# Another order table for a block-sparse attention with a gated FFN on one core

## The chip, the cores and the metric

The kernel runs on one core of a Trainium2 chip. A core has a matrix engine (TensorE, PE in the profile; its weight loads are listed as PEld), a vector engine (DVE), a scalar engine (ACT), a GpSimd engine (POOL) and a sync engine (SP). Each engine works through its own instruction stream strictly as written, and engines wait for each other through semaphores. DMAs are issued from SP, ACT or POOL and run beside the engines. The metric is the device time in microseconds (us). Three runs of the kernel before took 215.96, 216.22 and 216.23 us; the median is 216.22.

## The reference

Four sequences of 768 positions, 8 heads of 64 features. Attention is masked by blocks of 32 positions: a block sees its neighbours, the first and the last block, and three random blocks per row, which are given at run time.

```python
scores = scale * np.matmul(q, k.transpose(0, 1, 3, 2))
...
scores = np.where(mask, scores, -1000000000.0)
...
attn = attn / (np.sum(attn, axis=-1, keepdims=True) + 1e-09)
return np.matmul(attn, v).astype(np.float32)
```

The heads are put side by side (512 features) and go through a gated feed-forward layer with a convolution of width 3 over the positions:

```python
h = np.maximum(x @ w_in, 0.0)          # 512 -> 1024
...
conv_out += conv_w[k][None, None, :] * hp[:, k:k + S, :]
gate = 1.0 / (1.0 + np.exp(-conv_out))
return (h * gate @ w_out).astype(np.float32)   # 1024 -> 512
```

## The kernel before

**The work.** The kernel computes dense scores and adds the mask through 24 extra rows of the contraction (88 rows instead of 64). Heads are taken in 16 pairs; a pair's keys and queries lie in tiles `e` and `o` (even and odd 128-blocks), its values in `vt`. Queries are taken in halves of 384 positions, so there are eight half batches; the last one is cut into 256 and 128 positions. Scores come in 144 units of 128 keys x 1024 score columns:

- a score step (`s`, L742) is half a unit on PE and writes half of one of two `st` buffers; six matmuls make a unit;
- an exponential (`exp`, L753) on ACT turns a unit from `st` into one of six `pt` buffers;
- an `av` step (L775) on PE multiplies four 128-blocks of `pt` with the values into one of two `av` buffers; a ones column gives the row sums.

18 units make a half batch, and 4.5 units one pair of heads in it. Then follow, for each pair, `rcp` and `norm` on DVE (L692, L694), which divide by the row sums into `xtok`, and a transpose into `xT`: on PE with a copy behind it (`x_tr`, L713, `x_cp`) in the half batches 0, 1, 7 and 8 (the two pieces of the last count as 7 and 8), by a DMA from SP (`x_xb`, L703) in the others.

The feed-forward part of a half batch runs while the next half batch's attention runs: `f1` on PE (L864, eight groups of 128 hidden features, into one of two `mix` buffers), `relu` on ACT (L884) or DVE (L886) into `hE`, then for each pair of groups three `mul` steps (L916) and two `add` steps (L924) on DVE for the convolution, `tanh` on ACT (L963), `g1` and `g2` on DVE (L966, L971) into `gT`; then `f2` on PE (L802), a copy out of PSUM (`ev`, ACT or DVE, L336 or L340) and the output DMA from SP (L809). The last 128 positions have their convolution on PE (`conv`).

**Loads.** The first pair comes as float32 by DMAs from SP and ACT; all others are cast by DMAs issued from POOL (L239). Pairs 0 to 5 are turned by PE transposes (`k_tr`, L466; `q_tr`, L504) with copies behind them (`k_cp`, `q_cp`; L336 on ACT, L340 on DVE); pairs 6 to 15 by DMA transposes from SP (`xb`, L581) and a copy (`stg_cp`). The mask rows are copied from slot to slot on DVE (`m_h1`, `m_slot`, all L340). POOL holds its loads back with one-element copies (`pace`, L414 and L656), which wait for an exponential or an earlier load.

**What sets the order.** The source builds a graph of 1758 steps. Each names the engines that may run it, what it needs, and the buffers it takes and frees. No scheduler runs at build time: the string `ORDER` (L20) lists all steps, two characters for the step, then a letter for the engine where there is a choice (A for ACT, V for DVE), then a digit for each buffer that the step takes. `put_down` (L94, called at L987) reads the string from front to back and writes out each step's instructions. So the string fixes three things: the order of steps on each engine, the engine of each copy, `relu` and `ev`, and which buffer each step gets. A step that stands behind another on a different engine does not wait for it for that alone; it waits for what it needs and for its buffers.

Of the kernel before, what the change touches and what calls it, by code (L numbers as in the profile page):

```python
# [25 lines left out]
6o15yV6p690Z6d6e6q05+16t04v1P05/V6i6j6u6k06y16l6v14w6z160+6m06r06s6A26nV6D00S6E0X4xhW12l06F3hZ00/6I16JhX4y2m6K4
h+hYV06R06Sh/Vi316T5i4ii06W14z176Xik6wi5Ai00iji16Y04A2x11Q1i2V6/0701RAil4B6x2116B7417111SV6C75iq1290im6G762ic1
2aV47d0idir7ein7i14C2bV2z26H7j7f36L6M1is2c04DieV6U6V6Z7k46+7n06N12eV7oit2217p5722dV7s17t24V2n023V7u0737x0iu7y2q1
2oV02B02A7z1777G16O7H784E2pV2F27g0iv7h7L07926P0io4F7l2H37M7I27a7m7q7rip07v7w7A7N37B16QV17Q12rV7R7J0W7K7b07S47V0
7C07W2kV47O2sV7X57D2C4G82183107P7E17T8407cV8707FV887Uiw7Y8918c1ix2J12I7Z8d2yV0i602GV18e28h04H7+12N08i7/i7i918j3  # L30
4Ii8V2f0ia8508m12DV1ibA8nif08o4igiy28u0iz868a8vihAiA2P8z12Q18A8w5iBiO1iG3800iP8B0iC8E02K4J2t18biH8f8FiDiI8J12S8g
8kiJ8l81A8K8piE8q18G18x8yiK2g08CiF8D2RiL8H2iViQ2hV2OA28IiMiU02EViV8L2iN2T0iW2LV2iR2X2Y18R0iSA08SiX8T38W1iYV18X
i+18Y4i/2MV8/090j0Vj109158r2941958sj22Uj71960j3V9909a8Mjm0j409b12+9h1jo2/08t29i8Njnj89j2j58O0jp9m09nj9V8U0j6A8V
319r1jq9o3ja1jbju1jd0jvjrje8P9s9w0jcAjx8Z321308+92jfA93jwjj19t49xjC2jg0jhjyiZ9y5369E1js372jkjiV9798jz9cjE9F2u0jD
9d19G09J0jA9k9KjF9l9L19e19O1jt9p9q339PjlV9u2wA9T02vAjB9U9vk819Q2jK3k9jL9z9V3jGjY0393a29Y19f9A9ZjHjMa409g9H09IjN
9M9+4jZjOa59N9R8QjI9SjP9W3c9XjJa91aaa65kajQiT9/jRj+3bab09B2ae09Cj/2VV3af9Dk0A2kb3h2WVaj1ag1k20a11a2k33d0kcA3k4
2ZA3k5jS1k6V1a30jT34V4akjUal2ar0k1jVa01asjWA0ke0kfat3jXkh1kgV1kiaw135V3kkjAax3l3kn0ay4kokC03i0kk1kEaB0kpAklkDaC
kmAa7kFa8acaG1aD5kq0kGadaHkK1kt1kH3nahkMaL0kr3o13mkLaI0aikuksVamaMkvAkNkz03eaN1aT1kOaUkw1kS2ankPkx3skIkAao0kTaY0
aV2aZkJ1au0avazaAkyVaEkBAaFaJb11kVa+3b2aKkQl61apaOb34b60kRaqb7lc0kUb85be1k+3bfl7l03pbg0aP1kWaWbj0bkaQ2aXk/kXa/b0
b4bo1aRb5b9bl1bal1aSbh0bpldkYl2bq2bt0bikZbubmbb1l3lebcby1bzbv3bdl4bnl8l5brbsbA43qV0bG0bHk7l938V43fV1bI5lf3v3w1  # L40
laV2bL1bMlgA0bwbQ03rVli1bN0lh3gVljll0kdlkV3jA0lm3AbRlblnVbV1bWbS1lr1lG0lo0lIlsbX23x3B1lplHc10c2ltV3t1lqAbxc61lJ
c33c7bBbC1lO1lx1lylKc84cb0bJlzVcclD0lLlQcg1bKlP3ychlu1cd5bD0lRbObPlvbEbTci0lElMcl0bF1lSbUcmlwAbY3KlNct13L0lTlA1
lW2bZculYcn1c40lB3zlXc5c9calFVcv33Hcy03I2czb+2lUcelZlCAmg03PlVcA4cD1cfcEl+mh3Mb/cF2cjcI0ck3uV1ma1c0m23l/cJcom3
cp1cQ1cRcK5m4cw3CcxcBm5cCcGmbcS0m0m6cV0cHcLm1cM3NcWm7c+1cq1micrcX1c/m8mccscN0m9cT0cUd03d30cOd4mjcPd54cY3Zmd3+2
mkV1d81d9meV0mm03Q0da5dg03DV2mn3JV2mo3EV423OcZmfdhd1mpdi03W3Gdl1mqV3dmmy1dn1mz3/mB0mC3X0mAA0dq0mDVd2drms1mW0ds2
mtmX3Rdv1dwmYmudx3mZmE0mv40m+431d6d7mwV2mFm/dD0dbmGVdEdI1dc1n0dF4mH1n10mIdJdd2mJAmN04cde4d3dN0dK5mOn21df2dj41dO
n3dkmK1n4dP0mL494a1n5domxdpdS1dTmPVmMA4hdtdudX0dU13SV3dYdy3TVmQ1mRdZ2n6e314e4i0e4na2dzmT0nbe53mUmSVdG0e80dHe9n7
mVVdLed1dA1eeni3ea4nw1dBdMdQdRncdVef5dCdWd+ei04fndejnq0n8ek0e00eq1neer3Fd/1n9e6e744es1ev0njewnrnkex3eA1e1eb3VeB
ecnlege2nfehel4gem3YV3et0eF0nmeC4nx4ong4p2eueyen2eznheGnneK1eonyeH5eLepnonsnpeDeEeM045V4eS0eT4jnteU2eX1nuV0eYnz
eZ14bV4eI48eJnAV2eNf00mrf1eO1eP1f5146Vf23mlf6nC0eQ47nDf74nI1eR0nEVnJfd04qV0nKAfe4kV1nL0ff5nM3Ufi1nNVnvfjnF14lV  # L50
fk0eV4nnGo60eWnBfn0fonHAo8nR0fp2nSo7fs1n+1e+e/ftnTAn/nO1fu1nPo9fx0o0fyf3nQAf4o1nU0fz3fF1oafGf8f9o2nVfH4nX1oe2fg0
fK0offLo3nYogfhfP1fa0fM5flnZVfQfmfqo4frfbobfU0o5fvfcfVnWAohoA1fR0ocfwou0om3fAodfW2g01g1onfB1fIovoig21g50oog6oBop
ojfJfNfC2fOoqfSg73fTga1fDgbfXfYokfEg30org4g8olg9gj0gkgc4osoCotowgl5fZ1go1f+gpoxgq0f/gdoDoyV3gt0gugeoM0gv24mgf0oN
ggozoOoEA1oPoFgC1oQA0gDgh1gH0giA1gIoS0gE1oToV1oUV1gJ3oWgM1oXVgNp20gO4p3pe1p51pgp6p4Apfgm1gV0p7AgngrphoY0oZpigW
o+Agso/1pu0pjp0pwoG0pvp1Ag+1g/gX5oHpm2oIpnh00oJpogwh30pph4oKA2gxpxpb1h52gF0pqoLpcp80gy2pkoRgGpdAgKgzgLgPhc1prpy
# [962 lines left out]
```

## Time and profile before

| | |
|---|---|
| median of three runs | 216.22 us |
| span of the profiled execution, first to last instruction | 213.9 us |
| what lies around the span (difference of the two) | 2.3 us |
| PE busy | 203.6 us (95%) |
| ACT busy | 193.5 us (90%) |
| DVE busy | 186.6 us (87%) |
| POOL busy | 60.4 us (28%) |
| TensorE clock granted | 1.000 |
| start of the first score step, of the first exponential | 6.8, 7.9 us |
| start of the last exponential | 193.9 us |
| last instruction of PE, of DVE, of ACT | ends at 210.3, 208.4, 210.9 us |

The profiled execution's own time is its span, 213.9 us; its total is not listed apart from the three runs. Busy time is the union of the intervals of an engine's instructions. On PE neighbouring matmuls overlap in the record: `st` matmuls are listed with some 230 ns, but six of them take 0.44 us together.

### The profile page before, as it was taken

Reading aid. Unit: us, or ns where it says so; the run is one execution under the profiler, and the core shown is the slowest. Engines: PE = TensorE matmul, PEld = TensorE weight load, DVE = VectorE, ACT = ScalarE, POOL = GpSimd, SP = SyncE. Lnnn points to the kernel's source line nnn. Section 1 sums busy time; section 2 is a strip of 40 time slices with the busy share of each in tenths; the row PEclk is TensorE's granted clock in tenths of the full one; section 3 lists DMA queues with packets and bytes.
Section 4 is the critical chain, followed back from the end, with each engine's and each line's share of the span. In section 5 each row is a group of like instructions: output and inputs, shape, how many; then the busy total and the mean of one; then the engine's idle time right before and its main releaser. Section 6 shows DMA issues by size and latency. Waiting matters only on the chain.

```text
span 213.9 us, 6829 instructions
## 1 busy us (share of the span) xinstructions
PE 203.6 (95%) x2702; PEld 154.0 (72%) x2721; DVE 186.6 (87%) x577; ACT 193.5 (90%) x252; POOL 60.4 (28%) x117
## 2 busy tenths in 40 slices
PE   7899999999999999999999999999998999999991
PEld 3679978887677775778776766787786867785740
DVE  4899989999989994999999978999799939999980
ACT  6999999999899997999999977999999988997642
POOL 8883455733323130500327152730000000000000
PEclk9999999999999999999999999999999999999999
DMA  6999898998888977693599869699941130200205
GB/s 181 186 195 202 132 123 119 113 172 99 99 123 99 138 133 162 122 106 74 103 234 96 116 104 188 105 143 114 134 154 23 20 122 3 98 5 21 80 0 196
DMA packets 48935, 24.81 MB, mean 116 GB/s; under 512 B 35120, under 2 KB 45832, under 8 KB 48904
## 3 DMA queue, kind: packets, MB, share of 16 engines
q0 software_dynamic: 19728, 11.05, 43.0%
q1 hardware_dynamic: 28888, 13.05, 30.0%
q8 instruction: 21, 0.34, 0.7%
q10 hardware_dynamic: 288, 0.30, 0.4%
q14 instruction: 10, 0.08, 0.1%
HBM read 23.08 MB, written 6.29 MB: 137 GB/s over the span
## 4 chain that ended last, share of the span: by engine, by line
PE 66%; DVE 24%; ACT 6%; issue 3%; ACTq 0%; DVEq 0%
PE st L742 19%; PE mix L802 16%; PE mix L864 12%; PE av L775 10%; DVE m L916 9%; ACT pt L753 4%; DVE m L924 4%; DVE hE L886 3%; PE st L802 2%; PE mix L504 2%; PE av L230 2%; DVE xtok L694 1%; DVE gT L971 1%; DVE o L340 1%; DVE e L340 1%
## 5 line engine op out<-in xcount | busy, mean ns | idle before, releaser
L753 ACT ACTIVATE pt<-st 128x1024 bf16<-128x1024 f32 x144 | 141.3, 1027 | 5.6 <-PE st L742 4.2
L775 PE MATMUL av<-vt,pt 128*128 128x65 bf16 x1152 | 60.4, 193 | 0.2
L775 PEld LDWEIGHTS <-pt 128*128 128x128 bf16 x1152 | 52.3, 97 | 10.1
L864 PE MATMUL mix<-xT,winb 128*128 128x384 bf16 (+2 forms) x288 | 52.8, 308 | 0.3 <-DVE hE L886 0.3
L916 DVE TENSOR_SCALAR m<-hE,cw 128x382 bf16<-128x382 bf16 (+2 forms) x192 | 49.4, 320 | 0.2
L802 PE MATMUL mix<-woutb,gT 128*128 128x512 bf16 x157 | 44.6, 379 | 1.6 <-DVE gT L971 0.6
L742 PE MATMUL st<-o 88*128 88x128 bf16 (+1 forms) x240 | 44.5, 229 | 0.3 <-ACT pt L753 0.2
L742 PE MATMUL st<-o,e 88*128 88x128 bf16 (+1 forms) x228 | 44.2, 233 | 0.2 <-ACT pt L753 0.2
L742 PE MATMUL st<-e,o 88*128 88x128 bf16 (+1 forms) x224 | 42.5, 234 | 1.2 <-ACT pt L753 1.1
L742 PE MATMUL st<-e 88*128 88x128 bf16 (+1 forms) x208 | 41.8, 239 | 0.4 <-ACT pt L753 0.2
L742 PEld LDWEIGHTS <-o 88*128 88x128 bf16 x464 | 34.3, 97 | 8.9 <-issue 2.0
L742 PEld LDWEIGHTS <-e 88*128 88x128 bf16 x436 | 32.9, 97 | 9.0 <-issue 0.9
L924 DVE TENSOR_TENSOR m<-m 128x764 bf16<-128x764 bf16 (+2 forms) x64 | 33.8, 533 | 0.3
L864 PEld LDWEIGHTS <-winb 128*128 128x128 bf16 x288 | 24.2, 97 | 8.2 <-issue 0.8
L963 ACT ACTIVATE m<-m 128x764 bf16<-128x764 bf16 (+2 forms) x32 | 26.3, 821 | 1.9 <-DVE m L924 1.8
L414 POOL COPY pace<-pt 1x1 bf16<-1x1 bf16 x24 | 7.6, 315 | 58.9 <-ACT pt L753 58.8
L802 PEld LDWEIGHTS <-gT 128*128 128x128 bf16 x192 | 15.7, 97 | 11.7 <-DVE gT L971 2.3
L886 DVE TENSOR_SCALAR hE<-mix 128x384 bf16<-128x384 f32 (+2 forms) x30 | 16.4, 553 | 7.9 <-PE mix L864 7.6
L884 ACT ACTIVATE hE<-mix 128x384 bf16<-128x384 f32 (+2 forms) x34 | 16.5, 492 | 3.1 <-PE mix L864 2.2
L971 DVE TENSOR_TENSOR gT<-m,hE 128x764 bf16<-128x764 bf16 (+3 forms) x36 | 18.3, 511 | 0.5
L694 DVE TENSOR_TENSOR xtok<-av,rcp 128x384 bf16<-128x384 f32 (+2 forms) x36 | 18.2, 507 | 0.4
L239 POOL DMA_DIRECT2D nat<-in_q_dram x23 | 16.9, 734 | 2.4 <-issue 1.9
(88 smaller groups left out, 170.0 us busy)
## 6 DMA issues: line engine op xcount, KB each, us to landing
out_dram<-o2s SPq DMA_DIRECT2D x24, 256.0 KB, 2.6
nat<-in_k_dram POOLq DMA_DIRECT2D x15, 192.0 KB, 4.0
vn<-in_v_dram POOLq DMA_DIRECT2D x15, 192.0 KB, 5.5
nat<-in_q_dram POOLq DMA_DIRECT2D x6, 192.0 KB, 4.2
winb<-in_moe_w_in_dram POOLq DMA_DIRECT2D x2, 512.0 KB, 8.4
woutb<-in_moe_w_out_dram POOLq DMA_DIRECT2D x4, 256.0 KB, 4.8
nat<-in_q_dram POOLq DMA_DIRECT2D x9, 96.0 KB, 5.4
nq<-in_q_dram POOLq DMA_DIRECT2D x6, 96.0 KB, 4.5
```

The costliest lines, as they stand in the source:

```text
L239: return op(name, {eng: occ}, lambda e: on(e).dma_start(out=dst(), in_=src), prio, deps, dma=(kind, service), **kw)
L694: nm = op("norm", {"DVE": t_dps(128 * C)}, lambda e: nc.vector.tensor_tensor(out=xtok_t[xk.index][:, 0:C].rearrange("p c h d -> p h c d"), ...
L742: nc.tensor.matmul(out=st[:, 128 * x:128 * (x + n_)], lhsT=QK[kc % 2][s][0:88, 1, hh, kc // 2, :], rhs=QK[par][s][0:88, 0, hh, idx:idx + n ...
L753: nc.scalar.activation(out=pt_t[ptb.index], in_=st_t[stb.index], func=AF.Exp, bias=0.0, scale=0.125)
L775: nc.tensor.matmul(out=o[:, off:off + 65], lhsT=pt_t[ptb.index][:, 128 * x:128 * x + 128], rhs=V_t[vslot_b[P].index][:, hh, kc, 0:65], sta ...
L802: nc.tensor.matmul(out=acc(), lhsT=gT_t[gb.index][:, ffc, 128 * t:128 * t + 128], rhs=woutb[:, ffc, :], start=(ffc == 0), stop=(ffc == NFF ...
L864: nc.tensor.matmul(out=mix_t[hb.index][:, w1 * y:w1 * y + w1], lhsT=winb[:, fc, 128 * ffc:128 * ffc + 128], rhs=xT_t[xt_buf[n].index][:, f ...
L886: nc.vector.tensor_scalar(out=dst, in0=src, scalar1=0.5, scalar2=0.0, op0=ALU.mult, op1=ALU.max)
L916: nc.vector.tensor_scalar(out=m_t[cb.index][:, x, y, 0:w], in0=hE_t[heb.index][:, f0 + y, t0 + x:t0 + x + w], scalar1=cw[:, x, f0 + y:f0 + ...
L924: nc.vector.tensor_tensor(out=m[:, a_, :, 0:w], in0=m[:, a_, :, 0:w], in1=m[:, b_, :, 0:w], op=ALU.add)
L963: th = [op("tanh", {"ACT": t_act(2 * w) + 0.04}, lambda e, cb=cb, w=w: nc.scalar.activation(out=m_t[cb.index][:, 0, :, 0:w], in_=m_t[cb.in ...
L971: nc.vector.tensor_tensor(out=gT_t[gtb.index][:, f0:f0 + 2, t0:t1], in0=m_t[cb.index][:, 0, :, 0:w], in1=hE_t[heb.index][:, f0:f0 + 2, 1 + ...
```

## The change

All but the first 59 steps of the string are replaced: the same 1758 steps in another order, with other engines for some of them and other buffers. The 59 steps that stay are those up to and including the first score step. Nothing else in the source changes.

```diff
 ORDER = """
 000m010g0f0n0h02030410o0i0t050p0j0q0s060zA1t00k0r070AA0l081u18A1090v1F00a0b1aA0c1H20d0N0w01bA19V1c00O0xA1i11f0
-1dV00yA0e1jV1l11eV1kA1gA0R1o00E4K11hA4L0D4P01nA1mV1B14Q4M01v10u0Q0P1I1wV14R14U11xV4V1T11y00G4W24Z01V34+1zV0F1AA
-1W5214/30H532521p11sV05445b02715c1qV1C00I1rA4N0125g15d55h1DV4O4S1J14r1GV1281EV5i04T4X1KV25l05m134Y1LV1M05n15q14s
...
+1dV00yA0e1jV1l11eV1kA1gA0R1o00E4K11B11I4L4P04Q1v02730Q1nA0P0D0G1hV1mV1T11V14M04R10F4U14V1y11sV04Z04N04O4+4S4T
+4W24X5214Y1wV11zV1AA1xV534/31p15445b05c5d50J0I0H1rV0T1qV1C01DV1GV11EV0S4r284s1W5g15h1J15i0505l05m5n11M05q15r
...
```

Steps by engine, where there is a choice (a step not listed keeps its engine):

| step | ACT before | ACT after | DVE before | DVE after |
|---|---|---|---|---|
| relu | 34 | 31 | 30 | 33 |
| ev | 13 | 15 | 11 | 9 |
| x_cp | 5 | 7 | 11 | 9 |
| k_cp | 2 | 1 | 12 | 13 |
| q_cp | 7 | 6 | 19 | 20 |
| v_cp | 3 | 2 | 13 | 14 |
| stg_cp | 0 | 1 | 20 | 19 |

The numbers of instructions are the same on PE (2721 matmuls) and POOL and SP; DVE has 578 for 577, ACT 252 for 253.

The order on DVE from the first mask copy of head 1 on (`m_h1`) begins as follows; the number behind a tile is its buffer in the build, and the columns are the line, the operation, the tiles and the shape written:

```
before                                        after
L340 o_72<-o_72 24x2x384                      L340 o_72<-o_72 24x2x384
L340 e_67<-e_67 24x2x384                      L367 vt_80, L367 vt_79
L340 e_67<-av_64 64x256                       L340 e_67<-e_67 24x2x384
L290 ident_126<-ident 24x24                   L340 o_73<-o_72 24x1536
L367 vt_80, L367 vt_79                        L340 o_72<-av_63 64x384
L340 e_68<-mix_66 64x768                      L340 e_67<-av_64 64x256
L340 o_73<-mix_66 64x768                      L340 e_68<-e_67 24x1536
L340 o_73<-o_72 24x1536                       L340 vt_77<-m_110 128x12x64
L340 e_68<-mix_65 64x2x256                    L340 e_68<-mix_65 64x768
L340 e_68<-e_67 24x1536                       L340 e_68<-mix_66 64x2x256
L340 e_69<-e_67 24x1536                       L340 o_73<-mix_65 64x768
```

On ACT the copy `o_72<-av_63` (64x384, ahead of the first exponential) and the copy `e_67<-mix_66` (64x2x128, ahead of the sixth) are gone; both are on DVE. On PE the `av` steps of units 0, 1 and 2 stand between the score steps of units 3 and 4; before, they stood behind those of unit 5. On POOL the load of pair 3's keys is put ahead of pair 2's values, that of pair 4's keys, with a `pace` copy behind it, ahead of pair 3's queries, and both halves of the first weight matrix (`winb`) behind pair 3's values. Later in the table `norm` of the second pair of half batch 3 (counted from 0) stands behind that of the third pair, and on SP transposes and outputs are interleaved in another order.

More of the change, by code (lines that the diff above doesn't have):

```diff
@@ L26 @@
[L26 to L55, printed above, removed]
@@ new lines @@
+2LV22MVj0V2OA28Y4j2j3Vjm0jnjojp915941952Q32S2R4J2X2Y12t18Ij719909a9609b1j408M9h19i2+2/08Nj8j5jq8O08U08V8Z8+92
+9m09n9j23130j6Ajrj9V8Pju1jvjwjsjd1jx9r1jeja09s9397jbjt2T09o3jfAjy9t4jg1jcA369w09x9y5372989c9d19E19F8t29e1jC29k
+jj0jh9J09l9p9q9K9G09fjDjEjiV2U8Q9gjk9u9O19P9v9z2u1jz9L1iT9Q29A9T09UjlVjY09H09I9MjFjK32vA321iZ339V3jM2wVjGjL9Y1
+k819N9Z9R9S9Wa409Xa5jAjH9+4jNjBk9jZjOjP9B2jIjJa919/aaa65kaj+ab0jQjRae0kbkcA29Ca109D2VV32ZV3afaj1a01j/k0V3a22WA
+ag139k21k3k4jS0jTakjUjVk5ar0al234V4jWV0k6A1asa7ke0kfkh1kikgV1kjVkC0kDkE3a23c3bkFkGat3aw1axkn0aB0ay4a303d0a8ko
@@ L61 @@
+hP4pYApQ1hHqu2hnhJ0qihKqvqwpRpSho0hpA2pThI1hL0hMVhQhRqjpUA1hx0pPpVozhyAhS2hThU1q00hVAqR1qSqTAq1q60qkq7q8qO1qP
+r30q9qaq2Ar4qbr53qU0qVqWAqlqQVqcqdqm1qnr6qxq+1qoqX1q/r00r1qYqZAqpr2qqqI0qJqyr7qC1rd0reqDr81rf0qrqsqtqzqAr9ri0
+ro1rprjra3qKqEqBqFrgrhrbrcqGA3qLqHqMV2qNrqrrrsA1rtrkrlrmA0rn
 """
```

36 lines of the change are left out of this document (29 added, 7 removed).

## The prediction

> **What bounds the kernel now.** I read the page first (busy shares, slices, chain, groups), then the waits, then the span cut at the first exponential of each half batch, then the instructions around the point where the two tables part.
>
> ```profile
> PE 203.6 (95%) x2702; PEld 154.0 (72%) x2721; DVE 186.6 (87%) x577; ACT 193.5 (90%) x252; POOL 60.4 (28%) x117
> ...
> PEclk9999999999999999999999999999999999999999
> ...
> PE 66%; DVE 24%; ACT 6%; issue 3%; ACTq 0%; DVEq 0%
> ...
> L753 ACT ACTIVATE pt<-st 128x1024 bf16<-128x1024 f32 x144 | 141.3, 1027 | 5.6 <-PE st L742 4.2
> ```
>
> Three engines are nearly full at once. No single one carries the chain that ended last; it changes between PE and DVE and touches ACT.
>
> ```profile
> 25.90:46.00 20.10, 19.82 (x325) 16.77 (x322) 18.30 (x65) 19.60 (x24) 11.72 (x23) 1.00 1.05 120
> 46.00:70.20 24.20, 23.96 (x306) 17.95 (x306) 22.18 (x66) 23.53 (x31) 8.43 (x16) 1.00 0.90 117
> 97.00:120.10 23.10, 22.63 (x322) 17.51 (x323) 22.62 (x66) 22.98 (x30) 7.90 (x14) 1.00 0.81 130
> 120.10:143.90 23.80, 23.59 (x303) 17.50 (x304) 21.25 (x58) 20.91 (x25) 10.20 (x19) 1.00 0.94 130
> 193.90:213.90 20.00, 15.20 (x128) 9.08 (x127) 13.62 (x55) 10.09 (x22) 0.00 (x0) 1.00 0.21 79
> ```
>
> Each row is a stretch; its length, then busy PE, PEld, DVE, ACT and POOL. In 97 to 120 all three have under 0.5 us to spare; in 120 to 144 PE binds and ACT has 2.9 us free; in the last 20 us none is full, that is the tail.
>
> ```profile
> DVE hE L886 <- PE mix L864: 7.6, 8, 2.8
> ...
> ACT pt L753 <- PE st L742: 4.2, 10, 1.0
> ...
> ACT m L963 <- DVE m L924: 1.8, 3, 1.4
> ```
>
> No wait is large: the longest on ACT is 1.4 us. What a new order can win are many small waits, and it can make some.
>
> ```profile
> 7.22 0.76 ACT L336 COPY o<-av 64x384 bf16<-64x384 bf16 x2
> 7.88 2.84 ACT L753 ACTIVATE pt<-st 128x1024 bf16<-128x1024 f32 x3
> 8.95 0.22 PE L742 MATMUL st<-e,o 88*128 88x128 bf16 x1 [0.74 <-ACT pt L753]
> ...
> 12.85 0.37 ACT L336 COPY e<-mix 64x256 bf16<-64x256 bf16 x1
> 13.12 1.96 ACT L753 ACTIVATE pt<-st 128x1024 bf16<-128x1024 f32 x2
> ```
>
> Two copies stand ahead of the first exponential on ACT, one ahead of the sixth.
>
> **Work by engine.** PE's work is the same; POOL and SP issue the same DMAs. ACT gives up three `relu` (0.39 each, from start to next start), a `k_cp` (0.49), a `q_cp` (0.27) and a `v_cp` (0.80) and takes two `ev` (0.48), two `x_cp` (0.36) and one `stg_cp`. That copy of 64x1536 has no row on ACT; by exponentials (1024 columns, 0.92) and `ev` (512, 0.48) it is between 0.92 and, continued on their line, 1.36, and I take 1.36. Sum: -2.73 + 3.04 = +0.3, and with the cheaper shapes among them about 0. DVE changes by 0.2. So all that can move the time is waiting.
>
> **The start, walked by hand.** DVE after its mask copy (ends 7.4 with head 1's E copy behind it at 7.8) now does a slot copy (0.55), the copy taken from ACT (0.32), the query copy (0.24): 8.91. Then slot copy (0.55) and the value copy (0.75): 10.21. On ACT the first exponential needs the scores that end at 7.44 and starts at 7.5 instead of 7.88; the third needs score steps that wait for DVE's 8.91 and starts at 9.6 (before 9.7). Then the new order costs: `av` of unit 0 stands ahead of the second score step of unit 3 and waits for the values, 10.21, so exponential 3 (counted from 0) starts at 10.94 (before 10.89); unit 4 waits for pair 1's key and query copies, 10.21 + 0.47 + 0.33 + 0.47 = 11.48, so it starts at 11.98 (before 11.81). Without the ACT copy exponential 5 starts at 12.90 (before 13.12). Three slot copies, two query copies and two fills now hold `mix` until 13.8, so the next key transposes come at 13.85 and exponential 7 at 15.1 (before 15.19); DVE's copies for pair 2 end at 16.25 and exponential 9 starts at 16.97 (before 17.23). **Gain 0.3.**
>
> **DMAs moved.** Pair 3's queries, issued at 8.70 before, now stand behind pair 4's keys and a `pace` that waits for pair 0's queries, which landed at 11.3: issue about 11.9, with this kind's median of 5.4 us to landing 17.3. Their transposes ran at 19.0, by the walk 18.7: hidden, 1.4 us left of 4.1. Pair 2's values go behind one more load of 0.72 us, having 4.2 us to spare. The first weights move from 12.1 to about 14.3, landing (8.4) 22.7, first `f1` 28.6: hidden. Pair 0's second queries had landed 0.3 us before their transposes at 11.6; these now run near 11.8. SP's queue keeps its 20 + 20 transposes; the tightest `f1` (104.4, three us after its last `xT` issue) has 1.1 us more PE work ahead of it. Zero for all of these.
>
> **The middle.** For each half batch I add up, from the first unit to the next half batch's first, the durations of the steps that stand there on PE (between score steps) and on ACT (between exponentials), by the spacings in the trace: a unit of scores 0.44, four `av` matmuls 0.12, four `f1` 0.65, two `f2` 0.43, exponential 0.92, `tanh` 0.73.
>
> | units | from, us | took | PE before/after | ACT before/after |
> |---|---|---|---|---|
> | 0-18 | 7.9 | 18.0 | 14.8/15.0 | 17.1/16.8 |
> | 18-36 | 25.9 | 20.1 | 18.1/18.3 | 18.9/19.3 |
> | 36-54 | 46.0 | 24.2 | 22.2/21.7 | 23.1/21.9 |
> | 54-72 | 70.2 | 26.8 | 26.1/26.3 | 24.4/24.6 |
> | 72-90 | 97.0 | 23.1 | 21.3/21.7 | 22.7/22.3 |
> | 90-108 | 120.1 | 23.9 | 23.7/23.2 | 19.9/22.9 |
> | 108-126 | 144.0 | 22.2 | 20.8/21.0 | 21.4/20.7 |
> | 126-143 | 166.2 | 27.7 | 25.5/25.5 | 24.9/24.6 |
>
> The larger of the two, summed from unit 18 on, goes from 161.4 to 159.5: -1.9. With marks every 36 units it stays (0.0), every 9 it rises by 0.7. These are the ends; they differ in how much lead an engine may have over another, which no row gives, so I take their mean: **gain 0.4**. DVE has 1.2 to 4.3 us free in the same stretches but for 97 to 120.
>
> **The tail.** Behind the last score step PE has 16.2 before and 16.1 after; behind the last exponential ACT 8.8 and 8.5; behind the last `norm` DVE 9.4 and 9.2; `f2`, `ev` and output close it in the same order. **Gain 0.1.**
>
> **Sum.** Span 213.9 - 0.3 - 0.4 - 0.1 = 213.1; with 2.3 around it (216.22, the median, less the span) 215.4 us.
>
> **Rivals.**
> 1. *No net change.* The start's 0.3 is swallowed by the first stretch where PE binds (120 to 144) and the middle stays at its 36-unit sum: 216.2.
> 2. *Slower: `tanh` waits for DVE's adds and holds the exponentials behind it.* Place: units 66 to 92. Six of the eight `tanh` there start at most 0.12 us after the add that they need (89.06 after 89.03; those at 92.1, 97.9, 110.3, 113.4 and 121.3 alike). The new table has 0.8 to 2.7 us less ACT work ahead of the eight and 0.8 to 1.6 us more DVE work ahead of their adds. Where DVE did not do this extra work in its idle time before (3.7 us free between 70 and 97, mostly waits for `f1`), they come up to 1.6 later: 216.2 + 1.6 = 217.8. It decides once DVE's free time in that stretch is under 1.6. For it: chain pieces on DVE at 85.0 to 90.6 and 105.9 to 117. Against: those 3.7 us. If the same happens before units 136 and 139 (adds with 1.7 to 2.0 us more in front), another 1.0 is lost: 218.8.
> [...]
> 4. *Late loads.* Pair 3's queries took 6.2 us to land when issued at 8.70. At 11.9 + 6.2 = 18.1 they still come before 18.7; what goes beyond that is lost on the path: 1.5 us later than 18.7 makes the forecast's 215.4 into 216.9.
>
> **Chances.** Forecast, with the middle anywhere in its gain: 0.50. No net change 0.12. Rival 2: 0.30; rival 4 and the like in SP's queue: 0.06; clock: 0.02. Runs of one kernel differ by some 0.1%, so 0.2% (0.43 us) is about what can be told from no change. Faster 0.50, within 0.2% 0.12, slower 0.38. Low end: 0.5 at the start, 1.9 in the middle and a fifth of the 7.5 us that the stretches take beyond their larger load (1.5): 212.3. High end: rival 2 at both places, 218.8. For the forecast alone 213.5 to 215.8.
>
> **What would show it.** Right: first exponential near 7.5, the tenth near 17.0; the first exponential of half batch 3 (before 70.2) and of half batch 6 (144.0) 0.3 to 1 us earlier; the tail 20 us. Wrong: `tanh` with idle of over 2 us from adds in the waits, or the stretch from unit 72 to 90 over 23.6 us; idle on PE from `gT` above its 0.6.

## The result: 0.7% slower

The changed kernel takes 217.76 us (median of 20 runs, 217.12 to 219.56), the kernel before, run between them, 216.93 us. The ratio is **1.0069, 95% interval 1.0046 to 1.0092**: 1.0 to 2.0 us slower, where 0.8 faster was forecast. A later series of 12 gave 218.78 us and 1.0083 (1.0050 to 1.0117). One sentence is needed to read these numbers: the medians are over all executions and the ratios leave out the slowest ones, which are mostly the old table's (43 of its 149 in all series lie above 219.7 us, none of the new table's 32), so that 0.7% is the difference of undisturbed executions, while the means over all of them are 217.9 us before and 218.0 after in the first series, 217.9 and 218.7 in the later one.

The profiled execution after took 217.51 us, its span is 215.6 (before 213.9). The page of after, the lines that answer to those of before and one more, L802:

```profile
PE 204.8 (95%) x2700; PEld 155.2 (72%) x2721; DVE 186.6 (87%) x578; ACT 192.8 (89%) x251; POOL 61.0 (28%) x117
...
DVE 43%; PE 42%; ACT 10%; issue 4%; ACTq 0%; DVEq 0%
...
L753 ACT ACTIVATE pt<-st 128x1024 bf16<-128x1024 f32 x144 | 142.3, 1033 | 5.4 <-PE st L742 4.3
...
L802 PE MATMUL mix<-woutb,gT 128*128 128x512 bf16 x155 | 43.3, 379 | 2.5 <-DVE gT L971 1.5
```

The engines do nearly the same work as before. In the chain DVE's share has risen from 24% to 43% and PE's has fallen from 66% to 42%, and TensorE now waits 1.5 us for the DVE's gating products `gT`, 0.6 before. The same five stretches, cut at the first exponentials of the same half batches in after (columns: stretch, length, busy PE, PEld, DVE, ACT, POOL, clock, DMA share, GB/s):

```profile
26.50:47.60 21.10, 20.14 (x324) 17.01 (x321) 18.78 (x68) 19.69 (x25) 11.09 (x24) 1.00 1.02 124
47.60:70.70 23.10, 22.66 (x305) 17.25 (x303) 22.28 (x64) 22.28 (x29) 8.65 (x17) 1.00 0.85 106
98.50:121.20 22.70, 22.24 (x319) 17.53 (x323) 22.48 (x68) 22.53 (x29) 7.41 (x13) 1.00 0.67 120
121.20:145.90 24.70, 24.33 (x319) 18.22 (x320) 20.22 (x55) 23.65 (x30) 10.99 (x19) 1.00 0.94 128
196.10:215.60 19.50, 14.70 (x129) 8.91 (x128) 13.01 (x53) 9.58 (x22) 0.00 (x0) 0.98 0.26 95
```

Units 18 to 36 take 1.0 us more (21.1 for 20.1), units 36 to 54 1.1 less, 72 to 90 0.3 less, 90 to 108 0.8 more, the tail 0.5 less (the rows are cut at tenths of a microsecond). The list of waits of after (engine and line, what it waited for, sum, times, longest):

```profile
PEld L802 <- DVE gT L971: 3.2, 8, 1.0
...
ACT o L336 <- DVE e L340: 1.2, 2, 0.8
...
DVE o L340 <- ACT e L336: 0.9, 1, 0.9
...
ACT m L963 <- DVE m L924: 0.9, 3, 0.4
```

The list of before has, for TensorE's matmuls that wait for `gT` (1.5 us in the L802 row of after) and for copies on one engine that wait for copies on the other:

```profile
PE mix L802 <- DVE gT L971: 0.6, 2, 0.3
...
DVE e L340 <- ACT o L336: 0.3, 1, 0.3
```

New in size in after are the second and the third row, 2.1 us between copies on ACT and copies on DVE (0.3 in before); the fourth is shorter than it was. L336 and L340 are one helper, a copy on ACT or on DVE. A transposed query tile is copied in two halves, `q_cp`; where one half is on ACT and the other on DVE, the second waits until the first is done (in after it starts 0.03 us behind the first one's end, at 35.26 and at 41.11). Before has five such pairs too and after six, so it is not the split alone that costs, but what stands ahead of the first half and behind the second. In the timeline of after, DVE and then ACT (start, duration, instruction, idle time before it and what ended it):

```profile
33.81 0.54 DVE L916 TENSOR_SCALAR m<-hE,cw 128x382 bf16<-128x382 bf16 x2
35.26 0.42 DVE L340 COPY o<-mix 64x512 bf16<-64x512 bf16 x1 [0.91 <-ACT e L336]
```

```profile
39.29 1.02 ACT L753 ACTIVATE pt<-st 128x1024 bf16<-128x1024 f32 x1 [0.16 <-PE av L775]
41.11 0.37 ACT L336 COPY o<-mix 64x256 bf16<-64x256 bf16 x1 [0.79 <-DVE e L340]
41.38 1.02 ACT L753 ACTIVATE pt<-st 128x1024 bf16<-128x1024 f32 x1
```

At 35.26 the DVE has stood idle 0.91 us for ACT's half (`q_cp13`); it then works without a break to 41.1, so its half `q_cp18` comes late, and ACT waits 0.79 for it with `q_cp19`, and with `q_cp19` exponential 30. Before has one row of five exponentials there:

```profile
36.66 5.01 ACT L753 ACTIVATE pt<-st 128x1024 bf16<-128x1024 f32 x5
```

From exponential 24 to 30 before takes 7.25 us, after 8.62. (Steps are numbered from 0 in the order in which the kernel defines them; exponential u is unit u's.)

### The profile page after: what moved, and what is told of

It reads as the page before. It is cut to its first block, busy times and chain, and to the rows that moved or that the text cites. A ratio compares the mean times of both kernels' runs of the same rounds, so it can differ in the third digit from the quotient of the medians.

```text
span 215.6 us, 6829 instructions
## 1 busy us (share of the span) xinstructions
PE 204.8 (95%) x2700; PEld 155.2 (72%) x2721; DVE 186.6 (87%) x578; ACT 192.8 (89%) x251; POOL 61.0 (28%) x117
## 4 chain that ended last, share of the span: by engine, by line
DVE 43%; PE 42%; ACT 10%; issue 4%; ACTq 0%; DVEq 0%
DVE m L916 15%; PE mix L802 12%; PE st L742 11%; ACT pt L753 9%; DVE m L924 9%; PE mix L864 8%; DVE hE L886 5%; PE av L775 4%; DVE xtok L694 3%; DVE gT L971 3%; DVE o L340 2%; DVE e L340 2%; DVE m L966 2%; PE av L230 2%; PE st L802 2%
## 5 line engine op out<-in xcount | busy, mean ns | idle before, releaser
L775 PE MATMUL av<-vt,pt 128*128 128x65 bf16 x1152 | 58.2, 193 | 0.2
L775 PEld LDWEIGHTS <-pt 128*128 128x128 bf16 x1152 | 51.1, 97 | 8.8 <-issue 0.4
L864 PE MATMUL mix<-xT,winb 128*128 128x384 bf16 (+2 forms) x288 | 53.5, 308 | 0.4 <-DVE hE L886 0.3
L802 PE MATMUL mix<-woutb,gT 128*128 128x512 bf16 x155 | 43.3, 379 | 2.5 <-DVE gT L971 1.5
L742 PE MATMUL st<-e,o 88*128 88x128 bf16 (+1 forms) x224 | 43.4, 236 | 0.1
L742 PEld LDWEIGHTS <-e 88*128 88x128 bf16 x436 | 33.5, 98 | 10.0 <-issue 1.4
L802 PEld LDWEIGHTS <-gT 128*128 128x128 bf16 x192 | 16.1, 97 | 14.1 <-DVE gT L971 3.2
L414 POOL COPY pace<-pt 1x1 bf16<-1x1 bf16 x24 | 8.7, 361 | 61.4 <-ACT pt L753 61.4
L886 DVE TENSOR_SCALAR hE<-mix 128x384 bf16<-128x384 f32 (+2 forms) x33 | 18.1, 552 | 5.2 <-PE mix L864 5.2
L884 ACT ACTIVATE hE<-mix 128x384 bf16<-128x384 f32 (+2 forms) x31 | 15.5, 503 | 1.7 <-PE mix L864 1.1
```

Of the source, the lines that this page charges most:

```text
L742: nc.tensor.matmul(out=st[:, 128 * x:128 * (x + n_)], lhsT=QK[kc % 2][s][0:88, 1, hh, kc // 2, :], rhs=QK[par][s][0:88, 0, hh, idx:idx + n ...
L775: nc.tensor.matmul(out=o[:, off:off + 65], lhsT=pt_t[ptb.index][:, 128 * x:128 * x + 128], rhs=V_t[vslot_b[P].index][:, hh, kc, 0:65], sta ...
L802: nc.tensor.matmul(out=acc(), lhsT=gT_t[gb.index][:, ffc, 128 * t:128 * t + 128], rhs=woutb[:, ffc, :], start=(ffc == 0), stop=(ffc == NFF ...
L864: nc.tensor.matmul(out=mix_t[hb.index][:, w1 * y:w1 * y + w1], lhsT=winb[:, fc, 128 * ffc:128 * ffc + 128], rhs=xT_t[xt_buf[n].index][:, f ...
L886: nc.vector.tensor_scalar(out=dst, in0=src, scalar1=0.5, scalar2=0.0, op0=ALU.mult, op1=ALU.max)
```

## The experiments

A table entry can't be read, so the diffs write steps by name and number. Where a run puts one table's order behind the other's, the second gives the order of the steps that are left. The traces are compared by the start of the same exponentials, in us behind before's trace (start 7.88 for exponential 0):

| run | 0 | 9 | 24 | 36 | 60 | 84 | 114 | span | time | ratio (95%) |
|---|---|---|---|---|---|---|---|---|---|---|
| after | 0.7 | 0.6 | 0.3 | 1.6 | 1.3 | 1.8 | 1.8 | +1.7 | 217.76 | 1.0069 (1.0046-1.0092) |
| new_again | 0.8 | 2.2 | 1.9 | 3.6 | 3.3 | 3.8 | 3.8 | +3.8 | 218.78 | 1.0083 (1.0050-1.0117) |
| new18_old | -0.1 | 0.5 | 0.8 | 1.8 | 2.0 | 2.0 | 2.0 | +2.2 | 217.61 | 1.0026 (0.9989-1.0064) |
| new36_old | 0.9 | 1.8 | 1.5 | 2.9 | 3.1 | 3.1 | 3.1 | +3.2 | 218.32 | 1.0063 (1.0028-1.0098) |
| old36_new | 0.6 | 0.8 | 0.8 | 0.8 | 1.0 | 1.8 | 1.8 | +1.8 | 217.60 | 1.0002 (0.9966-1.0038) |
| old90_new | 0.4 | 0.3 | 0.3 | 0.3 | 0.3 | 0.3 | 1.9 | +1.8 | 218.77 | 1.0033 (0.9994-1.0072) |
| old9_new | 0.1 | 0.2 | 0.3 | 1.4 | 1.0 | 1.8 | 1.8 | +1.8 | 218.10 | 1.0079 (1.0050-1.0108) |
| new_q_one_engine | -0.5 | 1.7 | 1.4 | 3.2 | 2.9 | 4.6 | 4.6 | +4.6 | 219.55 | 1.0137 (1.0089-1.0186) |
| old9_new_q_g | 0.8 | 4.8 | 5.0 | 6.4 | 6.0 | 6.6 | 6.6 | +6.6 | 221.60 | 1.0157 (1.0087-1.0226) |
| old_q_two_engines | 0.3 | 2.1 | 2.2 | 4.2 | 4.2 | 4.2 | 4.2 | +5.0 | 219.61 | 1.0138 (1.0081-1.0195) |
| old_new12_60_old | -0.1 | 1.1 | 1.1 | 2.4 | 2.0 | 2.1 | 2.1 | +2.1 | 217.60 | 1.0028 (0.9981-1.0074) |
| new_old12_60_new | 0.8 | 2.2 | 1.9 | 2.1 | 2.1 | 3.9 | 3.9 | +3.8 | 218.72 | 1.0089 (1.0055-1.0122) |
| old_new60_84_old | -0.2 | 0.1 | 0.1 | 0.1 | 0.1 | 2.5 | 2.1 | +2.8 | 220.56 | 1.0141 (1.0076-1.0206) |
| new_q_dve_order | -0.5 | 0.4 | 0.1 | 1.4 | 1.0 | 1.8 | 1.6 | +1.6 | 217.34 | 1.0036 (1.0000-1.0072) |
| new_x_early | 0.9 | 2.0 | 1.7 | 3.3 | 2.9 | 4.2 | 4.2 | +4.1 | 218.74 | 1.0104 (1.0054-1.0153) |
| new_q_x | 0.8 | 0.9 | 0.6 | 1.3 | 0.9 | 2.2 | 2.2 | +2.1 | 217.62 | 1.0060 (1.0029-1.0091) |
| old9_new_q_x | 0.8 | 4.8 | 4.9 | 5.0 | 4.7 | 5.9 | 5.9 | +5.8 | 220.24 | 1.0038 (0.9995-1.0080) |
| new_q_t | -0.5 | 0.8 | 0.5 | 1.0 | 1.3 | 2.6 | 2.6 | +2.5 | 218.35 | 1.0081 (1.0050-1.0112) |
| old_warm | 0.3 | 0.6 | 0.6 | 0.6 | 0.6 | 0.6 | 0.6 | +0.6 | 216.86 | 1.0008 (0.9983-1.0034) |

A single mark moves by up to 1 us with what stands just ahead of an exponential; 24, 60, 84 and 114 are marks where the new and the old table have done within about 2 us of the same work on each engine (at exponential 60 after's DVE has done 1.3 us more than before's, its ACT 1.0 less), so their differences are no exact prices. What a run loses up to exponential 9, where it is more than about 0.8, is something else, told at the end; so read the rows by their steps from one column to the next.

**Where it is lost: the two tables put together.** Four runs.

```diff
 steps ahead of exponential 18 (new18_old) or 36 (new36_old)
-  old order
+  new order
 all steps behind: old order
```

> The new table for the steps listed before exponential 18, the old table for all others. Theory A (the loss is made where the new table has ACT's query copy wait for DVE, units 27 to 31; the start is not on the path): the same as before, ratio 0.998 to 1.002. The prediction's start term: 0.3 us faster, 0.9986, and the first exponential on record about 0.4 us earlier. Theory B (the new start costs): 1.003 or more.

> The new table up to exponential 36, then the old one. Theory A: carries the whole loss, 1.005 to 1.008, with exponential 36 at about 47.6 us of the span instead of 46.0. Rival (rival 2 of the prediction: tanh waits for DVE's adds in units 66 to 92): the same as before, 0.998 to 1.002. Theory C (the loss is spread over the whole table): 1.001 to 1.003.

```diff
 steps ahead of exponential 36 (old36_new) or 90 (old90_new): old order
 all steps behind
-  old order
+  new order
```

> The old table up to exponential 36, then the new one. Theory A: the same as before or faster, 0.995 to 1.002. Rival 2: the whole loss, 1.005 to 1.008. Theory C: 1.004 to 1.006.

> The old table up to exponential 90, then the new one. Theory A: the same as before, 0.997 to 1.002. Rival 2: nearly the same, since its place lies before the cut, 0.998 to 1.003. Theory D (the end loses: between exponential 126 and the last the new table's record is 0.5 us longer): 1.003 or more.

Behind the old order nothing is made up: old90_new keeps its 0.3 unchanged from exponential 9 to 90, new18_old its 2.0 from 45 to 126. In old36_new exponential 60 stands only 0.2 behind where 24 stood, in after 1.0: the stretch from 24 to 36 loses when it has the new order. But old90_new loses 1.6 from exponential 90 to 114, where after loses 0.6 between the same two marks and nothing from 84 to 114. So about 1.0 of it is a cost of the joint, and it warns that a part of an order can't be priced by putting it into another one; and that the whole loss is made at units 27 to 31 does not hold: old36_new, without it, stands at 1.8 from exponential 84 on, where after stands. By their times new36_old is slower than before, as theory A has it, and old36_new the same; new18_old and old90_new can't be told from before.

**The copies put on one engine, and the opposite.** Four runs on one chip.

```diff
 new_q_one_engine (new table)
-q_cp13 ACT
+q_cp13 DVE
-q_cp19 ACT
+q_cp19 DVE
```

> The new table with one thing changed: the two query copies `q_cp13` and `q_cp19` (the ACT halves of two transposed query tiles) go to the DVE, where their other halves are. In the new table's trace each pair of halves waits for itself: the DVE stands idle 0.91 us at 34.4 us until ACT's copy at 34.88 is done, and ACT stands idle 0.79 us at 40.3 us until the DVE's copy at 40.67 is done, with exponential 30 behind it. From exponential 24 to exponential 30 that trace has 8.62 us, the trace of before 7.25. Theory A (this is where the change loses): both idle times go, that stretch falls to 7.3 to 7.7, what follows keeps it, and the time falls by 0.6 to 1.0 to about 216.9. Theory D (absorbed: the new table's units 39 to 45 run 2.6 us faster than the old one's anyway and start from a later point): the stretch falls as well, but exponential 45 keeps its distance from exponential 24 (25.4 us) and the time stays at 217.5 to 217.9.

```diff
 old_q_two_engines (old table)
-q_cp12 ACT
 exp25 ACT
+q_cp12 ACT
 q_cp18 DVE
-q_cp19 DVE
+q_cp19 ACT
```

> The opposite transplant: the old table with only the new one's two splits: ACT's `q_cp12` goes behind exponential 25 (its other half on the DVE must wait for it), and `q_cp19` goes from the DVE to ACT behind exponential 29 (it must wait for the DVE's `q_cp18`). Theory A: the DVE stands idle about 0.9 us near 34 us and ACT 0.3 us or more near 40 us; from exponential 24 to 30 it takes 8.1 to 8.6 us instead of 7.25, everything later is shifted by as much, and the time is 0.8 to 1.3 over before: 217.2 to 217.8. Theory D: the later units take it up and the time is within 0.3 of before.

```diff
 old9_new
 steps ahead of exponential 9
-  new order
+  old order
```

> The old table up to exponential 9, the new one from there. In the run with the new table's first 18 units at the full clock, exponential 2 waited 0.31 us for scores held by a query copy on the DVE, and exponential 3 waited 0.39 us behind ACT's `q_cp7` for the DVE's other half `q_cp6`: 3.94 us from exponential 0 to exponential 3, against 3.01 in before. Theory B (the new start costs what the old one does not): exponential 0 to 9 takes about 9.3 us as in before, and the time falls by 0.4 to 0.7 against the new table, to about 217.1. Theory D (absorbed later): 217.5 to 217.9. Theory of my prediction (the new start gains 0.3): 218.0.

```diff
 old9_new_q_g = old9_new and
-q_cp13 ACT
+q_cp13 DVE
-q_cp19 ACT
+q_cp19 DVE
+g220 DVE
 add44 DVE
 g121 DVE
-g220 DVE
```

> Three edits at once to the new table: the old start up to exponential 9, the two query copies on the DVE, and the DVE's gating product `g220` two steps earlier (ahead of `add44` and `g121`), for which TensorE waited 0.92 us at 166.7 us. Theories A and B together: 1.0 to 1.7 shorter than the new table, 216.0 to 216.7, level with before or under it. Theory D: at least 217.2. The wait for `g220` should fall from 0.92 to 0.2; if the DVE's load sets that end, an equal wait appears one step later.

The transplant shows that such a wait costs: in old_q_two_engines the DVE waits

```profile
37.74 0.28 DVE L340 COPY e<-mix 64x256 bf16<-64x256 bf16 x1 [1.68 <-ACT o L336]
```

and from exponential 24 to 33 it loses 2.05 us, more than the 0.8 to 1.3 expected; the loss is 4.20 - 2.15 in every mark up to exponential 120 (behind it another 0.8 is lost, whose cause is open). Its wait is longer than after's 0.91, so it does not give the price of the waits in after. The cure in the new table failed in this form: at its old place in the table the copy `q_cp13` now stood ahead of three ready products on the DVE's queue, which idled 1.23 us for the transposes that it copies; from exponential 24 to 30 it took 8.07 us, not 7.3 to 7.7, and from 24 to 33 it lost 1.8 us, where after loses 1.4 and new_again 1.7. Behind exponential 60 it lost another 1.8, with a wait of 1.4 us on TensorE for a transposing transfer. With the old start, exponential 9 comes as before has it (+0.2), as theory B said, but the time did not fall: the new order behind it stands at 1.8 from exponential 84 on, where after stands. Half a microsecond at the start is gone by then; 1.6 us is not (new_again). old9_new_q_g ran nearly 5 us late from exponential 9 on, for the reason told at the end; its wait for `g220`, by the spacing of the matmuls, fell from 0.92 to 0.31, and TensorE's next wait, 0.59 for an exponential, followed at once. From exponential 24 to 84 it loses 1.6, as after does, so it shows no gain from the three edits.

**The stretches alone, and the copies put right.** Four runs on one chip.

```diff
 old_new12_60_old (old table)          new_old12_60_new: the same with old and new exchanged
 steps from exponential 12 to 60       old_new60_84_old: from exponential 60 to 84
-  old order
+  new order
```

> The old table, but with the new one's order between exponential 12 and exponential 60, places where both tables have done nearly the same work. In the run with the old table to exponential 9 and the new one behind, exponential 12 started 0.18 us before and exponential 60 1.01 us behind before's profile, and ACT stood idle 0.9 us more there, 0.79 of it ahead of `q_cp19`. Theory A2 (this stretch costs 0.7 to 1.2 us because ACT, which before keeps busy to 98% from 8 to 80 us, waits for the DVE's copies; the old table carries it to the end): exponential 60 is 0.7 to 1.3 later than exponential 12 has it, everything after is shifted by as much, and the time is 0.35 to 0.6% over before. Theory T (all that counts is the last part, where the new table makes the DVE wait at the batch changes): no loss, ratio 1.000 to 1.002.

> The mirror of it: the new table with the old order between exponential 12 and exponential 60. Theory A2: exponential 60 stands within 0.3 us of before's (start apart), ACT's idle time from 36 to 60 us is about 0.7 as in before and not 1.6. What the new table loses from 60 to 84 (0.6 to 0.8) remains: 216.9 to 217.3. Theory T: later units take the lead up, the end stays where the new table has it, 217.5 to 217.9.

> The old table with the new order between exponential 60 and exponential 84 alone. The new table's trace loses 0.55 to 0.8 us there: ACT waits 0.40 for scores ahead of exponential 48 and 0.39 for a DVE sum ahead of `tanh7` (77.8 us), and TensorE waits 0.46 to 0.6 at 107 to 112 us for a transposing transfer or a DVE step. If that holds, exponential 84 is 0.5 to 0.9 late, the old table carries it to the end, and the time is 0.25 to 0.45% over before. If the transfer is the gate only because of what comes ahead of it, there is no loss: 0.999 to 1.001.

```diff
 new_q_dve_order (new table)
-q_cp13 ACT
 mul1 DVE
 add0 DVE
 mul2 DVE
+q_cp13 DVE
 q_cp12 DVE
-q_cp19 ACT
+q_cp19 DVE
```

> The new table with `q_cp13` and `q_cp19` on the DVE once more, but `q_cp13` now directly ahead of `q_cp12`, behind the three products that the DVE has ready then: in the first form of this edit the DVE stood idle 1.23 us ahead of `q_cp13`, with ready products queued behind it. Theory A2: the DVE's idle 0.91 at 34.4 us and ACT's 0.79 at 40.3 go, exponential 24 to 33 takes 11.1 to 11.6 us (12.03 in the new table, 10.74 in before), and the time falls by 0.3 to 0.8 to 217.0 to 217.5. Theory D (the DVE is the bound there and is only loaded more): 11.9 to 12.3 us and no gain.

In old_new12_60_old exponential 60 is 0.97 later than exponential 24, and from there to the end nothing moves (2.02 to 2.07). That is theory A2's mark; the ratio of 1.0028 has an interval of 0.5% to both sides and adds little. ACT's wait is there again (0.91 ahead of the same copy). With the old order there, new_old12_60_new loses 0.15 from 24 to 60; then the joint at 60 costs 1.4 by exponential 66, and old_new60_84_old loses 2.4 where the new table itself loses 0.6. So 24 to 60 is a place of the loss by both runs, and 60 to 84 can't be judged by a transplant.

new_q_dve_order had the lowest time of the new table's forms, 217.34 us, ratio 1.0036 for 1.0069 and 1.0083; the intervals overlap, so a gain is not shown by the times. Its trace shows more. Exponential 30 stood 1.4 later, against before's, than exponential 24 in after; here it stands 0.4 earlier. But exponential 31 waits for its scores, and at exponential 33 the loss is back. ACT at exponential 31, then TensorE's wait between 39 and 42 us:

```profile
42.61 1.02 ACT L753 ACTIVATE pt<-st 128x1024 bf16<-128x1024 f32 x1 [1.04 <-PE st L742]
```

```profile
PEld L504 <- DMA nq<-in_q_dram: 1.3, 1, 1.3
```

In this execution the load of a pair's second half of queries (into `nq`, issued 35.11, landed 40.70) held TensorE for 1.3 us; in after it was issued at 34.48, landed at 38.75 and was read only at 40.30, 1.55 us later. The next series has the same repair with the load in time.

**The second stretch, and what adds up.** Four runs on one chip.

new_again is the changed kernel, unedited.

> The new table unchanged, once more, beside its edits: 217.2 to 218.2 us, 0.5 to 0.9% over before. In its trace exponential 60 should again stand 0.7 to 1.0 us further behind before's than exponential 24 does, and exponential 84 another 0.5 to 0.8, whatever its start was.

```diff
 new_x_early (new table)               new_q_x = this and new_q_dve_order's edit
+norm11 DVE                            old9_new_q_x = new_q_x with the old order
 g17 DVE                                 ahead of exponential 9
 g27 DVE
-norm11 DVE
 rcp15 DVE
+norm15 DVE
 g110 DVE
 g210 DVE
-norm15 DVE
 x_xb5 SP
+x_xb7 SP (transposing transfer of norm15's tokens)
 out4 SP
-x_xb7 SP
```

> The new table with the two last products of half batches 2 and 3 earlier on the DVE (`norm11` ahead of `g17`, `norm15` behind `rcp15` and ahead of `g110` and `g210`) and the second one's transposing transfer ahead of an output write on SP's queue. In the new table these transfers leave at 80.12 and 103.16 us, 5.7 and 3.5 us ahead of the first matmul that reads them, in before at 79.09 and 101.23, 5.4 and 4.1 ahead; traces with the new order there show waits of 0.4 to 1.6 us for them. Theory X (this is the second place of the loss): the transfers leave 0.6 to 1.0 us earlier, no wait for them is left, exponential 84 is 0.3 to 0.7 less late, and the time falls by as much, to 217.0 to 217.4. If something else sets exponential 84: no change within 0.2.

> Both repairs, the two query copies on the DVE behind its ready products and the earlier transfers: if the two losses are separate and add, 0.6 to 1.1 under the new table of the same chip, 216.6 to 217.1, 0 to 0.25% over before. If the second repair only moves the wait, it equals the run with the query copies alone (217.3).

> The old order up to exponential 9 as well, whose exponentials 2 and 3 do not wait for the DVE's copies: exponential 9 should come 0.2 to 0.4 us earlier than with the new start at the same clock. If the three losses add: 216.2 to 216.9, equal to before or a little under it. If they do not, the first 60 units take the lead up behind a load or a copy that does not move, and it is no faster than the run with the two repairs.

new_again came out slower than expected, 218.78 us for 217.2 to 218.2; its lag grew by 1.4 from 24 to 60 (0.7 to 1.0 expected) and by 0.6 from 60 to 84.

The copies: with the load in time the repair holds. ACT in new_q_x:

```profile
37.95 3.08 ACT L753 ACTIVATE pt<-st 128x1024 bf16<-128x1024 f32 x3
```

Exponentials 28, 29 and 30 run in one row, as in before. From 24 to 36 the lag grows by 0.65 in new_q_x and by 0.08 in old9_new_q_x, against 1.35, 1.74, 1.05 and 1.34 in after, new_again, old9_new and old_new12_60_old; from 24 to 60 by 0.3 and -0.3 against 1.0, 1.4, 0.7 and 1.0. That is theory A2 for this stretch; old9_new_q_x, nearly 5 us late for the reason told at the end, has its loads in time through that alone, so new_q_x is the cleaner of the two.

The transfers: theory X failed by the time and by its mark at exponential 84. They left 1.3 and 0.7 us earlier (78.83 and 102.42 in new_q_x, 80.12 and 103.16 in after), TensorE waits for none of them in these two traces, and from 60 to 84 both runs lose 1.2, twice what the new table loses. In new_x_early, as in these two, TensorE now waits for the product `g210`, past which `norm15` was moved, and exponential 77 comes 0.5 later for it (waits between 100 and 120 us):

```profile
PE mix L802 <- DVE gT L971: 0.4, 1, 0.4
```

Yet in other runs the transfer does hold TensorE. old9_new, old36_new and new_q_dve_order come to exponential 79 0.2 to 0.3 us ahead of after, and to exponential 80 0.3 behind it; TensorE waits in them 0.3 to 0.5 for a transposing transfer, in after for none. In old9_new:

```profile
PE mix L864 <- DMA xT<-xtok: 0.4, 1, 0.4
```

At exponential 84 all four stand at 1.8. So what was spared ahead of exponential 79 is lost again here, and that the copies' repair makes the whole kernel faster is not shown: from 24 to 84 new_q_dve_order loses 1.7 and new_q_x 1.5, after 1.5. Since in new_q_x the repair of the copies is worth what the earlier transfers cost, it (217.62) is no better than the copies alone. Beside new_again on the same chip it is 1.2 us lower by the median, but the intervals of the two ratios overlap.

**The last two.**

```diff
 new_q_t = new_q_dve_order's edit and
+s96 PE
+s97 PE
 f119 PE
-s96 PE
-s97 PE
+add14 DVE
+add15 DVE
 g15 DVE
-add14 DVE
 g25 DVE
-add15 DVE
```

> The new table with the query copies repaired as before and the two waits of ACT between exponential 48 and 60 removed: scores `s96` and `s97` go ahead of the FFN matmul `f119` on TensorE (ACT waited 0.40 for them at 63.3 us), and the DVE's sums `add14` and `add15` ahead of the gating products `g15` and `g25` (ACT's `tanh7` waited 0.39 at 77.8 us). Moving the transposing transfers earlier did not help, so theory X has fallen for this stretch. Theory W (what ACT waits here is what is lost): both waits go, exponential 84 is 0.2 to 0.6 less late than with the copies alone (1.76 behind before), and the time falls to 216.6 to 217.1. Rival P (TensorE, 98% busy there, or a product that now comes later, `g25` for `f221`, sets the end): exponential 84 as before the edit and 217.2 to 217.5.

```diff
 old_warm (old table)
 warm9 PE
+two matmuls of 128x256 on the warm-up tile
 w24 PE (six small matmuls)
+two matmuls of 128x256 on the warm-up tile
 k_tr0 PE
```

> The old table with four more warm-up matmuls of 256 columns, two ahead of the six small matmuls at 4.8 us and two behind them. In eight of the traces so far TensorE's matmuls fall back to half rate (107 ns for 128 columns instead of 56) at 5.6 us and stay there until 10 to 20 us, with either table, though their first 59 steps are equal; the first exponentials are then up to 1 us late, the tenth up to 4.8. If a longer warm-up sets the rate: exponential 0 is 0.2 to 0.6 us later than in before, none of the half rate is left behind 6 us, and the times lie together within 1 us, near 216.8, without those of 219 to 222. If not: the times spread as those of before, and are about 0.4 higher.

new_q_t refutes theory W: ACT's waits at exponential 48 and `tanh7` are gone, and TensorE waits for `g25`, which the sums were moved past, over 1 us; ACT stands idle 0.84 ahead of exponential 60 instead. It also waits 0.6 for a transposing transfer. From 60 to 84 it loses 1.3. Rival P has the sign, but it expected no change at exponential 84, and that came 0.9 later than with the copies alone. Up to exponential 36 this run, with its load in time, loses 0.5 from 24 on, as new_q_x does (0.65). Waits of that run between 76 and 84 us:

```profile
PE mix L802 <- DVE gT L971: 1.0, 1, 1.0
ACT pt L753 <- PE st L742: 0.8, 1, 0.8
```

old_warm: 216.86 us, ratio 1.0008 (0.9983 to 1.0034), eleven of its twelve runs between 215.93 and 217.63 and one at 219.52; the old table beside it had three of 17 at 220.75 to 221.08. Its mean over all runs is 217.0, the old table's in that series 217.5. Its median is no faster than before's; its mean is the lowest of all kernels here (after 218.0, new_q_dve_order 217.6). Exponential 0 came 0.3 later than in before, as expected, and its trace has no half rate behind 6 us; but eleven of the times lie within 1.7 us and not within 1, and one late run of 12 against three of 17 is too little to tell the two kernels apart.

## Why the prediction was wrong

**What bounds the kernel.** "Three engines nearly full at once" was right, and "what a new order can win are many small waits, and it can make some" was what happened. What I drew from it was not: that the waits can be left to a sum of loads.

**Work by engine.** Right for DVE, busy 186.6 in both. ACT has 0.7 less, where the sum had 0 to 0.3 more, though the one copy without a row took 1.47 for the 1.36 taken: the error is not in the direction of the loss.

**The start, gain 0.3: the mis-sized step is exponentials 2 and 3.** At full rate (56 ns from one 128-column score matmul to the next, 107 at half rate, as told at the end) the first exponential came at 7.39 (new_q_dve_order), 0.1 under the forecast 7.5. Then ACT in that run:

```profile
9.95 1.02 ACT L753 ACTIVATE pt<-st 128x1024 bf16<-128x1024 f32 x1 [0.63 <-PE st L742]
11.37 0.37 ACT L336 COPY o<-mix 64x256 bf16<-64x256 bf16 x1 [0.39 <-DVE e L340]
11.64 1.93 ACT L753 ACTIVATE pt<-st 128x1024 bf16<-128x1024 f32 x2
```

The query copy for unit 2 ended at 9.37, the walk had 8.91; exponential 2 came at 9.95 for 9.6. Exponential 3 came at 11.64 for 10.94: ACT's copy ahead of it (`q_cp7`) waits for the DVE's other half, and the walk knew no such wait, though both halves are in before's rows. The tenth exponential came at 17.6 (18.0 in new_q_t, also at full rate) and not at 17.0. At exponential 24 these two runs stand 0.1 and 0.5 behind before, old9_new with the old start 0.3, so by then this term is about 0 and not a gain of 0.3.

**DMAs moved, 0.** Right in after's profile, where no engine of the path waits for a moved load. In new_q_dve_order a load cost 1.3 us of TensorE's time; that was rival 4's kind, on a load the prediction did not look at. SP's queue, also put at zero, holds TensorE 0.3 to 1.4 us in other runs of the new order, in after not.

**The middle, gain 0.4: this step failed.** From exponential 18 to 143 after loses 1.7 us against before and new_again 2.1, where the larger of two loads per stretch was to gain 0.4. Three of its seven stretches came as the sums said (36 to 54: -1.2 forecast, -1.1 measured; 72 to 90: -0.4 and -0.3; 108 to 126: -0.4 and -0.3), but 18 to 36 came +1.0 for +0.4, 54 to 72 +1.0 for +0.2, 90 to 108 +0.8 for -0.5 and 126 to 143 +0.6 for 0. From exponential 24 to 84 the new table loses 1.5 us (1.9 in new_again). Busy ACT in two stretches at the same times, before and then after:

```profile
36.00:60.00 24.00, 23.57 (x367) 19.10 (x367) 21.82 (x66) 23.25 (x29) 10.11 (x20) 1.00 1.03 119
60.00:80.00 20.00, 19.71 (x262) 15.05 (x262) 19.27 (x57) 19.84 (x27) 5.62 (x11) 1.00 0.84 123
```

```profile
36.00:60.00 24.00, 23.03 (x356) 18.61 (x355) 23.39 (x72) 22.36 (x28) 10.44 (x22) 1.00 0.95 116
60.00:80.00 20.00, 19.63 (x269) 15.12 (x269) 19.52 (x57) 19.20 (x25) 5.87 (x11) 1.00 0.95 133
```

ACT, the fourth busy figure, has 0.9 and 0.6 us less in after. A load sum counts a copy as 0.3 us wherever it stands; that its other half is on another engine, and what stands behind it, is not in the sum; nor is DVE, which is as full as PE and ACT from 97 to 120. The mean of three markings was no bound either: the true value lay above all three ends (-1.9 to +0.7).

What is shown: of the 1.5 the first 1.0 is made between exponentials 24 and 60 (old_new12_60_old, new_old12_60_new), and the two split query copies make about half of it: with both on DVE and the load in time the stretch from 24 to 36 loses 0.65 and 0.5 (new_q_x, new_q_t) in place of 1.05 to 1.74. What is open: the rest of that, and the other 0.5, between 60 and 84. It is not the two transfers and not ACT's two waits, or not these alone: each repair brought a wait back one step later, at a DVE product that had been moved back, and runs that came earlier to exponential 79 waited for a transposing transfer. From 98.5 us to exponential 84 the DVE of after is busy 99%, from exponential 60 to there 82%; that it has no order that serves all is argued, not shown.

**The tail, gain 0.1.** Behind exponential 143 after needs 19.5 us, before 20.0.

**Rivals.** No. 2 had the sign, and the engine, DVE; its place and its price were wrong: `tanh` waits less for the adds than before (0.9 for 1.8), the stretch from 72 to 90 took 22.7 and not over 23.6. The sign that did come is the third one named, TensorE's idle time for `gT`, 1.5 for 0.6; of the signs of being right the first exponentials of half batches 3 and 6 came 0.5 and 2.0 later in after, not earlier. No. 1 priced a lost gain at zero, but a new order can also make waits. The chance of 0.02 for the clock was read from the granted clock. No execution here has a mean granted clock under 0.97; what the traces show in its place is half the matmul rate (107 ns for 56) at a granted clock of 1.00, as follows.

## What to carry to other kernels

An order for engines that are all nearly full can't be priced from loads: list every step pair that waits across engines, above all a tile whose two halves are copied on two engines, and look at what stands behind the waiting half in its engine's queue. Before a repair is believed, look one step further down the same queue and at the loads that the old delay had hidden: of five repairs here one shortened its own stretch, and none is shown to bring the kernel level with before. And with orders, compare whole tables by marks at nearly equal work, since a joint of two orders cost 1.0 to 1.8 us here by itself.
